# Sums and remainders of the last MLP's weight operands: from VectorE to GpSimd, in a kernel of three fused stages

## The chip, the cores and the metric

One core of one Trainium2 chip. The metric is the device time of one execution in microseconds. The kernel of before took 764.49, 761.42 and 763.99 us in three runs; the median is 763.99 us.

## The reference

Three blocks run one after the other, all in float32. `moe_w_*` and `moe2_w_*` arrive as 64-bit floats, so the kernel also has to turn them into 32-bit ones.

```python
# attention over 32 memory slots: q, k, v of (4, 8, 576, 64), phi of (4, 8, 576, 32)
a = softmax(phi, axis=2)
k_m, v_m = einsum('bhsm,bhsd->bhmd', a, k), einsum('bhsm,bhsd->bhmd', a, v)
x = softmax(q @ k_m.T / 8) @ v_m                 # then as (2304, 512)
x = ((x @ w_a) * (x @ w_b)) @ w_out              # 512 -> 1536 -> 512
h = x @ w2_in                                    # 512 -> 2048
out = maximum(0.01 * h, h) @ w2_out              # 2048 -> 512
```

## The kernel before

Every float32 product is made of three passes in the faster fp32r format: an operand is split into a high part (ScalarE rounds it to fp32r) and a low part (the remainder, value minus high part), and TensorE adds high x high, high x low and low x high.

The program has three stretches on TensorE. In the first (to about 87 us) the attention of the first batch and the first part of the gated MLP run. In the second (to 398 us) the rest of the attention and of the gated MLP run: `wp` (L741, the weights folded with v_m), `ab` (L792), `x1p` (L849). In the third (398 us to the end) the last MLP runs: `h` (L1250) and `o` (L1339, L1320). The last MLP is computed with a Strassen-Winograd scheme: 7 products of half-size blocks in place of 8. For it, sums of blocks of the weights w2_in and w2_out are needed beside the blocks themselves. All of these are made during the second stretch, written to DRAM (`a_scr`) and read back in the third into a ring.

`plan_pair` (L890) plans this work for one pair of 128-row or 128-column blocks, 8 pairs of w2_in ("in") and 8 of w2_out ("out"). For each of the two blocks of a pair there is a load of 512 KB into one of five `stage` places (L255), two ScalarE instructions that take the words of the 64-bit numbers apart (L262, L266) and one VectorE instruction that joins them (L274). Then come four sums per pair (`add`, L935: S1, S2 from S1, S3, S4 from S2, or T1 to T4). Seven operands are then split: ScalarE makes the high part (`high`, L958) and VectorE the low part (`low`, L961). Four stores (L975) follow. So a pair has 4 sums and 7 low parts, 11 VectorE instructions of 128x256 elements, and 16 pairs have 176. All their inputs lie in SBUF.

Four of the "out" pairs are planned early (`SOON`, mp 4 to 7, in the units u = 1 and u = 2 of the gated MLP); one pair waits for the last store of the pair before it, and so do the weights of the second half of the gated MLP after the last of them (`soon[-1:]`, L1011 to L1021). The other twelve pairs follow the last of these stores too (L1026 to L1030).

What comes when is not written by hand: `Plan.order` (L79) is a list scheduler that runs when the program is built. Every step has an engine and a planned cost (`t_dve`, `t_act`, for TensorE a cost per product), the lags between engines are a table (`LAG`), and the due times are passed backwards from TensorE's steps. The planner takes the step that can start first on any engine, and among those that can start equally early on one engine the one that is due first. The order that comes out is fixed: each engine executes its instructions in that order and waits, where an input isn't there, with all that is queued behind. The DMAs of the plan go through one queue, that of SP. On ScalarE the plan's queue also holds the copies that free PSUM banks (`copy`, L809), the high parts of W (L754) and of G (L828); on VectorE the low parts of W (L760) and G (L832) and the products of a and b (L814).

GpSimd has only some memsets and the identity matrix at the start.

Of the kernel before, what the change touches and what calls it, by code (L numbers as in the profile page):

```python
# [9 lines left out]
F32 = mybir.dt.float32  # L10
F32R = mybir.dt.float32r
# [3 lines left out]
ALU = mybir.AluOpType  # L15
AX = mybir.AxisListType

PE, DVE, ACT, DMA = "PE", "DVE", "ACT", "DMA"


class Step:
# [19 lines left out]
class Plan:  # L41
# [4 lines left out]


    LAG = {(PE, PE): 0.0, (DVE, DVE): 0.13, (ACT, ACT): 0.02, (DVE, PE): 0.3}
    LAG.update({(DMA, e): 2.0 for e in (PE, DVE, ACT)})
    LAG.update({(e, DMA): 1.7 for e in (PE, DVE, ACT)})  # L50
    LAG[DMA, DMA] = 2.0
    TICK, BUSY = 3.413, 3100

# [25 lines left out]
    def order(self, idle=None):  # L79

        for x in reversed(self.steps):
            for y in x.then:
                x.latest = min(x.latest, y.latest - self.lag(x, y) - x.cost - x.early)
        for x, r in self.rank.items():
            x.latest = r
        cols = defaultdict(float)

        def slow(t):
            return 1.0 if cols[int(t / self.TICK) - 1] >= self.BUSY else 2.0

        def count(t, cost, share):
            cols[int(t / self.TICK)] += cost * 2400 * share

        blocks, made = [0.0, 0.0], [0]

        def fetched(x):

            return blocks[min((made[0] + x.n - 1) // self.BLOCK, len(blocks) - 1)]

        def issue(x, t):  # L100
            made[0] += x.n
            while made[0] >= self.BLOCK * (len(blocks) - 1):
                blocks.append(t + (self.FETCH if t < self.START else self.FETCH_ALONE))

        free = {PE: 0.85, DVE: 1.0, ACT: 1.0, DMA: 0.8}
        ready = {e: [] for e in free}
        for x in self.steps:
            if not x.waits:
                ready[x.engine].append(x)
        out, left = [], len(self.steps)  # L110
        while left:
            best = None
            for e in free:
                can = []
                for x in ready[e]:
                    at = max(x.ready, free[e], fetched(x) if e == PE else 0.0)
                    if x.take:
                        places = sorted(self.places[x.take[0].pool])
                        if len(places) < len(x.take):
                            continue  # L120
                        at = max(at, places[len(x.take) - 1][0])
                    can.append((at, x))
                if can:
                    first = min(at for at, _ in can)
                    at, x = min((c for c in can if c[0] <= first), key=lambda c: c[1].latest)
                    if best is None or at < best[0]:
                        best = at, x
            if best is None:
                raise RuntimeError("the plan is stuck")
            at, x = best  # L130
            if x.engine == PE and idle is not None:
                until, fillers = idle
                for cost, emit in fillers:
                    while free[PE] + cost * slow(free[PE]) < at and free[PE] + 2 * cost < until:
                        y = Step(PE, cost, emit, n=4)
                        y.start = free[PE]
                        issue(y, y.start)
                        count(free[PE], cost, 1.0)
                        free[PE] += cost * slow(free[PE])
                        out.append(y)  # L140
            ready[x.engine].remove(x)
            left -= 1
            x.start, end = at, at + x.cost * (slow(at) if x.engine == PE else 1)
            if x.engine == PE:
                count(at, x.cost, 0.8)
                issue(x, at)
            free[x.engine] = end
            for h in x.take:
                place = min(self.places[h.pool])
                self.places[h.pool].remove(place)  # L150
                h.place = place[1]
            for h in x.give:
                h.users -= 1
                h.until = max(h.until, end + (1.7 if h.pool == "stage" else 0.2))
                if not h.users:
                    self.places[h.pool].append((h.until, h.place))
            for y in x.then:
                y.waits -= 1
                y.ready = max(y.ready, end + self.lag(x, y))
                if not y.waits:  # L160
                    ready[y.engine].append(y)
            out.append(x)
        return sorted(out, key=lambda x: x.start)


def t_dve(n):

    return 0.1 + n / 950


def t_act(n):

    return 0.08 + n / 1000
# [3 lines left out]
def kernel(  # L177
# [25 lines left out]
    nc = tc.nc  # L203
# [21 lines left out]
    scale = 1.0 / float(D) ** 0.5  # L225
    PASSES = ((0, 0), (0, 1), (1, 0))

    act, dve, pe, dma = nc.scalar, nc.vector, nc.tensor, nc.sync

    keep = ctx.enter_context(tc.tile_pool(name="keep", bufs=1))  # L230
    p_att_cm = tc.tile_pool(name="att", bufs=1, side="right")
# [658 lines left out]
    def plan_pair(kind, mp, due, after, soon):  # L890
# [35 lines left out]
        for n, ops in enumerate(sums):  # L926
            before, users = plan.slot(f"ob{n}")
            for i, (name, x, y, op) in enumerate(ops):

                def add(name=name, x=x, y=y, op=op, n=n, i=i):  # L930
                    if ("t", n) not in c:
                        c["t", n] = keep.tile([128, 2, 2, 128], F32, tag=f"ob{n}", name="S")
                    x, y = (c[z] if isinstance(z, str) else a(*z) for z in (x, y))
                    c[name] = c["t", n][:, i]
                    dve.tensor_tensor(out=c[name], in0=x, in1=y, op=op)  # L935

                need = [made[z] for z in (x, y) if isinstance(z, str)]
                give = [holds[z[0]] for z in (x, y) if not isinstance(z, str)]
                uses = [users] + [made[z].users for z in (x, y) if isinstance(z, str) and made[z].users is not users]
                made[name] = plan.add(DVE, t_dve(256), add, js + before + need, give=give, uses=uses)  # L940
                made[name].users = users
        for i, part in enumerate(parts):
            hold = Hold("stage", 1) if soon else None
            tag = None if soon else f"X{i}" if inner else f"R{i % 2}"
            before, users = ([], []) if soon else plan.slot(tag)
            lows = []
            for o, name in enumerate(part):

                def parted(o, x, i=i):
                    t = c["out", i][:, o]  # L950
                    return t[:, :, x] if inner else t[:, x].rearrange("p (a c) -> p a c", a=2)

                def high(i=i, o=o, name=name, hold=hold, tag=tag, part=part, parted=parted):
                    if o == 0:
                        shape = [128, len(part), 2, 2, 128] if inner else [128, len(part), 2, 256]
                        pool, to = (keep, f"stage{hold.place}") if hold else (p2[0], tag)
                        c["out", i] = pool.tile(shape, F32R, tag=to, name="a_out" if inner else "w2o")
                    act.activation(out=parted(o, 0), in_=src(name), func=ACTF.Copy)  # L958

                def low(o=o, name=name, parted=parted):  # L960
                    dve.tensor_tensor(out=parted(o, 1), in0=src(name), in1=parted(o, 0).bitcast(F32), op=ALU.subtract)  # L961

                direct = name[0] == letter
                need = js if direct else [made[name]]
                uses = [users] if direct else [users, made[name].users]
                hi = plan.add(ACT, t_act(256), high, need + before + lows, uses=uses, take=None if o else hold)
                lows.append(plan.add(
                    DVE, t_dve(256), low, [hi], uses=uses, give=[holds[int(name[1]) - 1]] if direct else ()
                ))

            def store(i=i, part=part):
                shape = [128, len(part), 2, 2, 128] if inner else [128, len(part), 2, 256]
                t = scr.tile(shape, F32, tag=f"{kind}{mp}_{i}", name="a_scr")
                (a_scr if inner else o_scr)[mp, i] = t
                dma.dma_start(out=t, in_=c["out", i].bitcast(F32))  # L975

            kept = plan.add(DMA, 0.73 * len(part), store, lows, uses=[users], give=[hold] if hold else (), due=due)
            (a_kept if inner else o_kept)[mp, i] = kept
            ends.append(kept)
# [507 lines left out]
```

## Time and profile before

| what | value |
|---|---|
| runs | 764.49, 761.42, 763.99 us, median 763.99 |
| profiled execution, its own time | 764.37 us |
| its span, first to last instruction | 762.5 us |
| TensorE matmul busy | 750.5 us, 98% |
| VectorE busy | 549.1 us, 72% |
| ScalarE busy | 423.7 us, 56% |
| GpSimd busy | 1.2 us, 9 instructions |
| granted TensorE clock, mean | 0.997 of 2.4 GHz |

The span is what the profiler saw between the first and the last instruction; the time of the execution is 1.87 us longer. Busy time of an engine is time in which at least one of its instructions was recorded as running. Records of neighbouring instructions on VectorE and ScalarE overlap, so the distance from start to start says more on their rate than the duration of one. GpSimd stands as POOL in the rows, VectorE as DVE, ScalarE as ACT, TensorE as PE, its weight loads as PEld, the queue of DMA issues as SPq.

### The profile page before, as it was taken

What the parts mean: (1) busy time and instruction counts of PE and PEld (TensorE: products, weight loads), DVE (VectorE), ACT (ScalarE), POOL (GpSimd) and SP (SyncE); (2) the same over time, 40 slices, a digit from 0 to 9 for tenths busy, and PEclk for the clock granted to TensorE, in tenths of its full rate; (3) what the DMA queues carried; (4) which work ended last, traced back from release to release, by engine and by line L of the source; (5) the groups of instructions that cost most, each with busy time, mean ns of one, the idle gap of its engine ahead of it and who ended that gap; (6) DMA issues with size and microseconds to landing.
All of it is one profiled execution on the core that took longest, in us unless ns stands there. A gap on an engine that the chain in (4) does not pass through costs nothing.

```text
span 762.5 us, 16527 instructions
## 1 busy us (share of the span) xinstructions
PE 750.5 (98%) x6462; PEld 709.8 (93%) x6462; DVE 549.1 (72%) x1082; ACT 423.7 (56%) x894; POOL 1.2 (0%) x9
## 2 busy tenths in 40 slices
PE   8999999999999999999999999999999999999996
PEld 5599898899898989898999999999999999999996
DVE  5795697786737988897856756976656966756683
ACT  4894575676857676675624455534344734444440
POOL 0000000000000000000000000000000000000000
PEclk9999999999999999999999999999999999999998
DMA  9972547364715596859746777778897788896375
GB/s 312 337 284 88 188 153 264 122 240 152 258 58 166 188 328 229 300 183 328 298 139 221 262 250 250 248 248 255 274 298 253 248 250 248 281 300 205 126 235 139
DMA packets 86926, 175.41 MB, mean 230 GB/s; under 512 B 8000, under 2 KB 35136, under 8 KB 86848
## 3 DMA queue, kind: packets, MB, share of 16 engines
q1 hardware_dynamic: 86608, 174.16, 68.8%
q8 instruction: 51, 0.84, 0.5%
q10 hardware_dynamic: 240, 0.20, 0.1%
q14 instruction: 27, 0.22, 0.1%
HBM read 140.25 MB, written 34.08 MB: 229 GB/s over the span
## 4 chain that ended last, share of the span: by engine, by line
PE 95%; DMA 2%; SPq 1%; DVE 1%; ACT 1%; issue 0%; ACTq 0%
PE h L1250 23%; PE o L1339 22%; PE x1p L849 21%; PE ab L792 20%; PE wp L741 3%; DMA stage<-in_moe_w_a_dram 1%; PE sc L624 1%; PE km L480 1%; PE qT L596 1%; PE warm L1184 1%; PE o L1320 0%; SPq L1375 0%; PE aT L691 0%; DMA w2o<-a_scr 0%; DVE AT L706 0%
## 5 line engine op out<-in xcount | busy, mean ns | idle before, releaser
L1339 PE MATMUL o<-w2o,S 128*128 128x256 f32 x1476 | 198.1, 282 | 0.0
L1339 PEld LDWEIGHTS o<-w2o,S 128*128 128x128 f32 x1476 | 193.0, 190 | 0.0
L792 PEld LDWEIGHTS ab<-AT,W 128*128 128x128 f32 x1152 | 154.2, 188 | 14.9 <-issue 4.2
L849 PE MATMUL x1p<-G,wo 128*128 128x288 f32 x1152 | 163.0, 298 | 0.0
L792 PE MATMUL ab<-AT,W 128*128 128x288 f32 x1152 | 160.8, 297 | 1.0 <-DVE W L760 0.7
L849 PEld LDWEIGHTS x1p<-G,wo 128*128 128x128 f32 x1152 | 154.6, 188 | 6.0 <-DVE x L870 2.5
L1303 DVE TENSOR_TENSOR S<-g,S 128x384 fp32r<-128x384 f32 x168 | 92.9, 556 | 78.5 <-ACT S L1302 78.2
L1302 ACT ACTIVATE S<-g 128x384 fp32r<-128x384 f32 x168 | 87.6, 521 | 99.6 <-PE o L1339 97.4
L1250 PE MATMUL h<-T,ring 128*128 128x384 f32 x720 | 142.2, 336 | 0.0
L1250 PEld LDWEIGHTS h<-T,ring 128*128 128x128 f32 x720 | 121.3, 189 | 0.0
L1250 PE MATMUL h<-B,ring 128*128 128x384 f32 x288 | 57.5, 337 | 0.0
L1293 DVE TENSOR_TENSOR g<-g 128x384 f32<-128x384 f32 x96 | 52.6, 554 | 4.2 <-ACT g L1260 3.0
L814 DVE TENSOR_TENSOR g<-a_sb,ab 128x288 f32<-128x288 f32 x96 | 43.0, 451 | 14.7 <-PE ab L792 10.2
L262 ACT ACTIVATE stage<-stage 128x512 f32<-128x512 f32 x68 | 46.4, 683 | 8.0 <-DMA stage<-in_moe_w_out_dram 3.2
L1250 PEld LDWEIGHTS h<-B,ring 128*128 128x128 f32 x288 | 48.3, 188 | 0.1
L760 DVE TENSOR_TENSOR W<-wp,W 128x512 fp32r<-128x512 f32 x48 | 32.3, 686 | 20.2 <-ACT W L754 19.9
L266 ACT ACTIVATE stage<-stage 128x512 int32<-128x512 uint32 x68 | 46.2, 679 | 0.0
L809 ACT COPY a_sb<-ab 128x288 f32<-128x288 f32 x96 | 38.0, 396 | 12.8 <-PE ab L792 12.3
L754 ACT ACTIVATE W<-wp 128x512 fp32r<-128x512 f32 x48 | 27.9, 597 | 24.5 <-PE wp L741 18.7
L832 DVE TENSOR_TENSOR G<-g,G 128x576 fp32r<-128x576 f32 x48 | 36.2, 755 | 4.6 <-ACT G L828 4.2
L1360 DVE TENSOR_TENSOR C<-C,o 128x768 f32<-128x768 f32 x32 | 30.2, 953 | 12.7 <-PE o L1339 11.3
L1260 ACT ACTIVATE g<-U 128x384 f32<-128x384 f32 x36 | 18.8, 522 | 33.4 <-DVE U L1275 23.7
(108 smaller groups left out, 673.1 us busy)
## 6 DMA issues: line engine op xcount, KB each, us to landing
w2o<-a_scr SPq DMA_DIRECT2D x168, 256.0 KB, 3.5
ring<-a_scr SPq DMA_DIRECT2D x72, 512.0 KB, 4.3
stage<-in_moe_w_out_dram SPq DMA_DIRECT2D x28, 512.0 KB, 5.6
a_scr<-w2o SPq DMA_DIRECT2D x24, 512.0 KB, 5.5
a_scr<-a_out SPq DMA_DIRECT2D x24, 512.0 KB, 5.7
stage<-in_moe_w_in_dram SPq DMA_DIRECT2D x16, 512.0 KB, 4.9
stage<-in_moe_w_a_dram SPq DMA_DIRECT2D x12, 512.0 KB, 6.7
stage<-in_moe_w_b_dram SPq DMA_DIRECT2D x12, 512.0 KB, 6.2
```

Of the source, the lines that this page charges most:

```text
L262: act.activation(out=x, in_=x, func=ACTF.Prelu, scale=2.0 ** -112, alpha=2.0 ** 32)
L266: act.activation(out=self.lw, in_=self.lw.bitcast(U32), func=ACTF.Copy, scale=7.249 / 2.0 ** 32, bias=0.25)
L792: pe.matmul(out=c[x, n][:, :HS], lhsT=W[b, f][:, hw, g, 128 * x:128 * x + 128], rhs=AT[b][:, g, ha, n * HS:(n + 1) * HS], start=(g == 0 an ...
L809: act.copy(c["sb"][:, n], c[0, n][:, :HS])
L814: dve.tensor_tensor(out=c["g"][:, n], in0=c["sb"][:, n], in1=c[1, n][:, :HS], op=ALU.mult)
L832: dve.tensor_tensor(out=t[:, 1], in0=c["g"], in1=t[:, 0].bitcast(F32), op=ALU.subtract)
L849: pe.matmul(out=c[n][:, :HS], lhsT=wo_t[f][:, hw, 128 * m:128 * m + 128], rhs=G[b, f][:, hg, n], start=(f == fs[0] and (hw, hg) == PASSES[0]),
L1250: pe.matmul(out=out, lhsT=ring[i % 2, part][:, o, kp, hw], rhs=x[:, hx], start=fresh and kp == 0 and (hw, hx) == PASSES[0], stop=kp == 1 a ...
L1293: dve.tensor_tensor(out=t, in0=x, in1=y, op=op)
L1302: act.activation(out=t[:, 0], in_=src, func=ACTF.Copy)
L1303: dve.tensor_tensor(out=t[:, 1], in0=src, in1=t[:, 0].bitcast(F32), op=ALU.subtract)
L1339: pe.matmul(out=acc[chain][:, 256 * u:256 * u + 256], lhsT=s[:, hs, 128 * u:128 * u + 128], rhs=t[:, ht], start=fresh and q == 0 and u != ...
```

## The change

GpSimd becomes a fifth engine of the planner with a cost function of its own, and the 4 sums and 7 low parts of every pair are planned and issued on it. Nothing else of the computation changes: the high parts stay on ScalarE, the joins on VectorE, the stores on SP's queue. Since the planner is given other costs and another engine, it may put every step of the plan elsewhere.

```diff
-PE, DVE, ACT, DMA = "PE", "DVE", "ACT", "DMA"
+PE, DVE, ACT, POOL, DMA = "PE", "DVE", "ACT", "POOL", "DMA"
...
-    LAG.update({(DMA, e): 2.0 for e in (PE, DVE, ACT)})
-    LAG.update({(e, DMA): 1.7 for e in (PE, DVE, ACT)})
+    LAG.update({(DMA, e): 2.0 for e in (PE, DVE, ACT, POOL)})
+    LAG.update({(e, DMA): 1.7 for e in (PE, DVE, ACT, POOL)})
...
-        free = {PE: 0.85, DVE: 1.0, ACT: 1.0, DMA: 0.8}
+        free = {PE: 0.85, DVE: 1.0, ACT: 1.0, POOL: 2.0, DMA: 0.8}
...
+def t_pool(n):
+
+    return 0.15 + n / 460
...
-    act, dve, pe, dma = nc.scalar, nc.vector, nc.tensor, nc.sync
+    act, dve, pe, dma, pool = nc.scalar, nc.vector, nc.tensor, nc.sync, nc.gpsimd
...
-                    dve.tensor_tensor(out=c[name], in0=x, in1=y, op=op)
+                    pool.tensor_tensor(out=c[name], in0=x, in1=y, op=op)
...
-                made[name] = plan.add(DVE, t_dve(256), add, js + before + need, give=give, uses=uses)
+                made[name] = plan.add(POOL, t_pool(256), add, js + before + need, give=give, uses=uses)
...
                 def low(o=o, name=name, parted=parted):
-                    dve.tensor_tensor(out=parted(o, 1), in0=src(name), in1=parted(o, 0).bitcast(F32), op=ALU.subtract)
+                    pool.tensor_tensor(out=parted(o, 1), in0=src(name), in1=parted(o, 0).bitcast(F32), op=ALU.subtract)
...
                 lows.append(plan.add(
-                    DVE, t_dve(256), low, [hi], uses=uses, give=[holds[int(name[1]) - 1]] if direct else ()
+                    POOL, t_pool(256), low, [hi], uses=uses, give=[holds[int(name[1]) - 1]] if direct else ()
                 ))
```

The planned cost of one of these instructions goes from t_dve(256) = 0.1 + 256/950 = 0.37 us to t_pool(256) = 0.15 + 256/460 = 0.71 us. These are numbers of the planner's table, not measurements.

## Rows read from the trace of the kernel before

**Rows 1.** The page, part 4: shares of the chain that ended last.

```profile
PE 95%; DMA 2%; SPq 1%; DVE 1%; ACT 1%; issue 0%; ACTq 0%
```

**Rows 2.** Three stretches: us; busy us of PE, PEld, DVE, ACT, POOL; PEclk, DMA share, GB/s.

```profile
0.00:87.00 87.00, 81.64 (x1091) 64.15 (x1092) 61.21 (x116) 55.02 (x113) 1.24 (x9) 1.00 0.72 246
87.00:745.00 658.00, 658.00 (x5300) 635.64 (x5300) 482.75 (x958) 367.62 (x779) 0.00 (x0) 1.00 0.70 230
745.00:762.50 17.50, 10.82 (x75) 9.98 (x73) 5.15 (x9) 1.05 (x2) 0.00 (x0) 0.89 0.53 140
```

**Rows 3.** PE's waits, whole span: us in total, times, longest us.

```profile
PE aT L691 <- DVE AT L706: 0.8, 1, 0.8
...
PE mxT L416 <- DVE mx L406: 0.6, 1, 0.6
```

**Rows 4.** The moved sums (L935) in two stretches: DVE busy us (instructions).

```profile
98.00:182.00 84.00, 6.25 (x16) 1.00 0.59 207
248.00:377.00 129.00, 19.24 (x48) 1.00 0.73 262
```

**Rows 5.** The moved low parts (L961) in the same stretches.

```profile
98.00:182.00 84.00, 11.14 (x28) 1.00 0.59 207
248.00:377.00 129.00, 32.22 (x82) 1.00 0.73 262
```

**Rows 6.** All engines in the later of these stretches, columns as in rows 2.

```profile
248.00:377.00 129.00, 129.00 (x1036) 119.97 (x1036) 112.55 (x260) 87.80 (x203) 0.00 (x0) 1.00 0.73 262
```

**Rows 7.** DVE by time, one pair's last sums and low parts: start us, us.

```profile
161.19 0.71 DVE L274 SCALAR_TENSOR_TENSOR stage<-stage 128x512 int32<-128x512 int32 x1
...
164.14 1.12 DVE L961 TENSOR_TENSOR w2o<-S,w2o 128x256 fp32r<-128x256 f32 x3
165.15 0.45 DVE L961 TENSOR_TENSOR w2o<-stage,w2o 128x256 fp32r<-128x256 f32 x1
...
166.18 0.44 DVE L961 TENSOR_TENSOR w2o<-stage,w2o 128x256 fp32r<-128x256 f32 x1
```

**Rows 8.** GpSimd's groups by shape: busy us, mean ns of one.

```profile
L1177 POOL MEMSET kk<- 128x256 f32 x2 | 0.6, 313 | 0.0
masks.py:199 POOL TENSOR_SCALAR_AFFINE_SELECT ident<-ident 128x128 f32<-128x128 f32 x1 | 0.3, 293 | 0.0
masks.py:197 POOL MEMSET ident<- 128x128 f32 x1 | 0.2, 204 | 0.0
```

**Rows 9.** DVE's groups by shape, 248 to 377 us, two with both inputs in SBUF.

```profile
L274 DVE SCALAR_TENSOR_TENSOR stage<-stage 128x512 int32<-128x512 int32 x22 | 15.1, 687 | 0.1
L832 DVE TENSOR_TENSOR G<-g,G 128x576 fp32r<-128x576 f32 x19 | 14.3, 751 | 1.5 <-ACT G L828 1.5
```

**Rows 10.** ACT by time: a high part that waited for a sum.

```profile
260.67 0.42 ACT L958 ACTIVATE w2o<-S 128x256 fp32r<-128x256 f32 x1 [3.20 <-DVE S L935]
```

**Rows 11.** DVE by time: a low part of W.

```profile
279.62 0.68 DVE L760 TENSOR_TENSOR W<-wp,W 128x512 fp32r<-128x512 f32 x1
```

**Rows 12.** PE by time, the block whose second half uses this W.

```profile
278.41 6.64 PE L792 MATMUL ab<-AT,W 128*128 128x288 f32 x48
```

**Rows 13.** SP's queue by time: the last stores of pairs, the ring's loads.

```profile
375.25 3.80 SPq L975 DMA_DIRECT2D a_scr<-a_out  x4
379.10 1.29 SPq L1053 DMA_DIRECT2D ring<-a_scr  x2
```

**Rows 14.** DMA issues, 370 to 400 us: KB each, median us to landing.

```profile
ring<-a_scr SPq DMA_DIRECT2D x2, 256.0 KB, 4.4
```

**Rows 15.** PE by time, the start of the last MLP.

```profile
398.48 2.24 PE L1250 MATMUL h<-B,ring 128*128 128x384 f32 x12
```

**Rows 16.** SP by time, the first weight load behind the early pairs.

```profile
168.20 1.90 SPq L255 DMA_DIRECT2D stage<-in_moe_w_a_dram  x1
```

**Rows 17.** PE by time, the first product that needs these weights.

```profile
226.35 1.09 PE L741 MATMUL wp<-wab,vblk 64*32 64x512 f32 x16
```

More of the change, by code (lines that the diff above doesn't have):

```diff
@@ L955, in high @@
                         shape = [128, len(part), 2, 2, 128] if inner else [128, len(part), 2, 256]
-                        pool, to = (keep, f"stage{hold.place}") if hold else (p2[0], tag)
-                        c["out", i] = pool.tile(shape, F32R, tag=to, name="a_out" if inner else "w2o")
+                        home, to = (keep, f"stage{hold.place}") if hold else (p2[0], tag)
+                        c["out", i] = home.tile(shape, F32R, tag=to, name="a_out" if inner else "w2o")
                     act.activation(out=parted(o, 0), in_=src(name), func=ACTF.Copy)
                 def low(o=o, name=name, parted=parted):
-                    dve.tensor_tensor(out=parted(o, 1), in0=src(name), in1=parted(o, 0).bitcast(F32), op=ALU.subtract)
+                    pool.tensor_tensor(out=parted(o, 1), in0=src(name), in1=parted(o, 0).bitcast(F32), op=ALU.subtract)
                 direct = name[0] == letter
```

## The prediction

> **What bounds the kernel now.** I read the chain of waits first: 95% of it is TensorE [rows 1]. Then the busy time by stretches [rows 2]: from 87 to 745 us TensorE is busy for 658.00 of 658.00 us, at a granted clock of 1.00, the level of 2.4 GHz. Its idle time lies outside: 87 - 81.64 = 5.4 us before 87 us, and 17.5 - 10.82 = 6.7 us in the tail. Then its waits: VectorE is named as releaser in four before the tail, from 0.8 down to 0.6 us, 2.7 us in sum [rows 3]; all of them end before 87 us. So in the stretch of 658 us TensorE waits for nothing, and what it has to do there isn't touched by the change.
>
> Next I looked for the instructions that move. The sums fall into two stretches, 16 at 98 to 182 us and 48 at 248 to 377 us [rows 4], the low parts with 28 and 82 [rows 5]; that is 174 of 176, and all of them lie within TensorE's 658 us. In the later stretch VectorE is busy for 112.55 of 129 us and ScalarE for 87.80, while TensorE is busy for all of it [rows 6]. VectorE is nearly full there, and still not what TensorE waits for.
>
> **What the change removes.** Three low parts in a row start at 164.14 and the next at 165.15 us, so one occupies VectorE for 0.337 us [rows 7]. 176 of them are 59 us, 130 x 0.337 = 43.8 us of it in the later stretch. On the path that sets the end this is worth 0 us: the work that hides it is TensorE's unbroken stream, and the bound of the gain is what TensorE waits for VectorE there, 0 us.
>
> **What it adds.** No row of before shows a GpSimd instruction with two inputs. From below: a write alone of the same size takes 0.313 us [rows 8]. In between an estimate: two memsets of 128 and 256 elements take 204 and 313 ns, so 0.85 ns per element and 95 ns fixed; one instruction with a read and a write takes 293 ns for 128 elements, (293 - 95) / 128 = 1.55 ns, so a read adds 0.70 [rows 8]. Two reads and a write of 256 elements are then 95 + 256 x 2.25 = 671 ns. From above: the same plus a wait for the whole of the longest VectorE instruction with two SBUF inputs in this stretch, 0.751 us [rows 9], 1.42 us. I take 0.67 us, because it rests on the only rows of this engine. GpSimd then has 44 x 0.67 = 29 us of work in the 84 us of the early stretch and 130 x 0.67 = 87 us in the 129 us of the later one, 68%. The planner books 0.707 us for each, 92 us. At the lower end it would be 41 us, at the upper 185 us, more than there is.
>
> Each moved step is one instruction and issues no DMA. GpSimd's own queue holds nothing else after the first microseconds, so nothing there is passed or held up. But the waits change: ScalarE waits for a sum before it makes its high part, and SP's queue waits for the low parts before a store. Behind the waiting ScalarE instruction stand the copies that free PSUM banks, the high parts of W and G and the word instructions; behind a store stand the loads of the next pair. One wait of this sort exists already: a high part waits 3.20 us for a VectorE sum [rows 10], and TensorE goes on. That was while `x1p` ran; while `ab` runs the cover is thinner. The low part of a W ends at 279.62 + 0.68 = 280.30 us [rows 11], and the products that use it are the second 24 of a block that begins at 278.41 us with 6.64 / 48 = 0.138 us each, so at 281.7 us [rows 12]. That is 1.4 us of slack. A ScalarE that loses more than this against its plan stops TensorE.
>
> At the end of the stretch the cover is thick: the last stores of the pairs are issued by 375.25 + 3.80 = 379.1 us, the last two ring loads by 380.4 us [rows 13], 4.4 us later they land [rows 14], at 384.8 us, and the last MLP starts at 398.48 us [rows 15], 13.7 us of slack. The early pairs release the weight loads at 168.20 us [rows 16], and the product that needs these weights starts at 226.35 us [rows 17]. From the last join to the last low part a pair takes 166.62 - 161.19 = 5.4 us on VectorE [rows 7]; on GpSimd 11 x 0.67 = 7.4 us, 2 us later. This vanishes in 58 us.
>
> **The sum.** Gain on the path 0 us, loss on the path 0 us as long as GpSimd keeps to the planner's 0.707 us: 764.37 us, the profiled execution's own time (its span of 762.5 us and 1.87 us around it). The median of the three runs is 763.99 us, 0.4 us lower, and the runs differ by 3.1 us. About 0.5%, 3.8 us, is what a measurement of this kernel can tell from no change.
>
> **One rule against the change.** Rows first: in the later stretch VectorE has 22 joins of 687 ns and 19 low parts of G of 751 ns, 29.4 us with both inputs in SBUF [rows 9]; no row shows GpSimd reading beside them. Of such pairs the Trainium skill, "SBUF — State Buffer", section "Who interferes with whom", says that the second read port of VectorE is GpSimd's, and that of a VectorE instruction with two SBUF inputs and a GpSimd instruction that reads SBUF the second to come is held until the first is done. By it the time would be that of the first rival; without it that of the sum. Nothing in this trace decides between them.
>
> **The rivals.**
>
> GpSimd becomes the pace (slower). Place: 248 to 377 us. If the two engines shut each other out, GpSimd stands still while one of these VectorE instructions runs. It is at work 68% of the time, so 0.68 x 29.4 = 20 us are added to its 130 instructions, 0.154 us each: 0.825 us, 0.118 us over what the planner booked, 15.3 us in all. If the pairs keep their present pace, the planner leaves GpSimd 129 - 92 = 37 us idle, and this swallows it. If the planner, with VectorE relieved, packs the pairs as closely as GpSimd's booked cost allows, little idle time is left to swallow it; ScalarE falls behind by up to 15.3 us, and TensorE stops for what is over 1.4 us: 13.9 us, 778 us. With half of it swallowed, 7.7 - 1.4 = 6.3 us: 771 us. It decides from where GpSimd's mean instruction exceeds 0.707 us while it works without a break. For it: VectorE's 87% here show that pairs are packed onto whatever is free. Against it: a wait of 3.2 us that cost nothing, and a planner that books 5% more than my estimate. VectorE, held in its turn for some 0.34 us by 68% of 41 instructions, loses 9.5 us and stays far below what it gave up. At the upper bound of 1.42 us the stretch would need 185 us, 56 us more than it has.
>
> The planner gives back early waits (faster). With other costs every step may be put elsewhere. If the four early waits for VectorE went, 761.7 us, still within 0.5%; all 5.4 us of early idle time, 759.0 us. Against it: no moved instruction comes before 98 us.
>
> The change doesn't do what it says: the inputs of all moved instructions lie in SBUF, and I see nothing that would keep them off GpSimd. The time would be 764.4 us too, without a chance of its own.
>
> **How the numbers follow.** No measurable change: 0.61. GpSimd's pace: 0.33, from 768.3 us (just over 0.5%) to 778 us and the far bound beyond, about 0.13 of it above 772 us. Faster: 0.06, nearly all below 761.4 us. The range of 761.4 to 772 us leaves out some 0.18; its lower end is the lowest run of before. Taken alone, the likeliest case has 761.4 to 768.
>
> **What would show it.** Right: 176 GpSimd instructions of 0.6 to 0.75 us from start to start, VectorE's busy time lower by some 60 to 70 us (its records are longer than its occupation), TensorE busy without a break from 87 to 745 us, `h` beginning at 398 us within 1 us. Wrong by the first rival: waits of ScalarE for GpSimd of over 1.4 us, with TensorE waiting for W or a PSUM bank just behind them, and `h` later by the loss. The prediction is also wrong if TensorE's products get another pitch than 0.138 us, which I hold fixed, or if GpSimd's low parts come so late that the ring's loads land after 398 us.

## The result, and the profile after the change

The changed kernel takes 768.14 us in the median (767.73 to 769.80), beside 762.78 us of the kernel before on the same chip. The ratio of the two kernels' runs is 1.0062 with a 95% interval of 1.0042 to 1.0083: slower by some 4.7 us (the medians, of four runs each, lie 5.4 us apart). The profiled execution took 767.73 us, with a span of 765.9 us.

The page of the changed kernel, parts 1 and 4, answers to [rows 1]:

```profile
PE 753.5 (98%) x6462; PEld 711.2 (93%) x6462; DVE 506.5 (66%) x906; ACT 424.1 (55%) x894; POOL 148.7 (19%) x185
...
PE 82%; DMA 5%; POOL 4%; issue 3%; DVE 2%; ACT 2%; SPq 0%; POOLq 0%; DVEq 0%; ACTq 0%
```

GpSimd is now in the chain that ended last, and TensorE's share fell from 95% to 82%. Busy time by stretches, columns as in [rows 2]; the third and fourth lines answer to [rows 2, 6]:

```profile
0.00:240.00 240.00, 234.79 (x2679) 205.48 (x2680) 155.91 (x288) 158.14 (x341) 36.15 (x53) 1.00 0.60 203
...
87.00:240.00 153.00, 152.83 (x1589) 140.97 (x1588) 94.69 (x172) 103.14 (x228) 34.90 (x44) 1.00 0.53 179
...
87.00:745.00 658.00, 655.90 (x5262) 631.80 (x5261) 436.81 (x777) 365.94 (x775) 147.43 (x176) 1.00 0.69 229
...
248.00:377.00 129.00, 127.29 (x1006) 116.42 (x1005) 78.75 (x126) 85.41 (x194) 103.48 (x121) 1.00 0.73 259
```

TensorE is no longer unbroken, and the break lies in the later stretch: 1.7 us of idle time there, 0.2 us between 87 and 240 us. From 248 to 377 us VectorE fell from 112.55 to 78.75 us busy and GpSimd rose from 0 to 103.48 us, 80% of the stretch. The granted clock is 1.00 as before. TensorE by time, beside [rows 15]:

```profile
402.96 1.21 PE L1255 MATMUL h<-B,ring 128*128 128x384 f32 x6
```

The last MLP begins 4.48 us later than at 398.48, and from there on nothing is lost: its first and last product lie 323.04 us apart, 323.03 before. So nearly all of the loss is in the pairs' later stretch. (The two profiled executions lie only 3.4 us apart, because the tail behind the last `h` is 1.1 us shorter in this one: 765.9 - 726.00 against 762.5 - 721.51 us.) GpSimd's groups by shape, busy us and mean ns of one:

```profile
L940 POOL TENSOR_TENSOR S<-stage 128x256 f32<-128x256 f32 x32 | 29.9, 938 | 226.8 <-DVE stage L279 225.3 <-POOL w2o L966 1.4
L966 POOL TENSOR_TENSOR a_out<-S,a_out 128x256 fp32r<-128x256 f32 x32 | 26.7, 855 | 0.1
L966 POOL TENSOR_TENSOR w2o<-S,w2o 128x256 fp32r<-128x256 f32 x32 | 26.0, 820 | 7.3 <-ACT w2o L963 7.3
```

The records average 805 to 953 ns over all seven groups. From start to start, where one follows the other without a wait, the median is 0.71 us and the mean 0.84 us. So half of them take about what the planner books (0.707 us), and the rest draw the mean 0.13 us above it. VectorE's two operations with both inputs in SBUF, 248 to 377 us, answer to [rows 9]:

```profile
L279 DVE SCALAR_TENSOR_TENSOR stage<-stage 128x512 int32<-128x512 int32 x23 | 19.5, 848 | 12.0 <-ACT stage L271 9.4 <-POOL S L940 1.2 <-POOL w2o L966 1.2
...
L837 DVE TENSOR_TENSOR G<-g,G 128x576 fp32r<-128x576 f32 x18 | 18.1, 1006 | 5.8 <-ACT G L833 5.7
```

They were 687 and 751 ns long and are 848 and 1006 ns now, with nothing in their own shape or operands changed.

**How VectorE stops TensorE.** One place, three engines by time: first VectorE, then GpSimd, then TensorE.

```profile
320.83 1.05 DVE L1098 TENSOR_TENSOR T<-x 128x384 f32<-128x384 f32 x1
321.81 1.10 DVE L1098 TENSOR_TENSOR T<-x,x 128x384 f32<-128x384 f32 x1
322.83 1.23 DVE L279 SCALAR_TENSOR_TENSOR stage<-stage 128x512 int32<-128x512 int32 x1
323.99 0.74 DVE L837 TENSOR_TENSOR G<-g,G 128x576 fp32r<-128x576 f32 x1
324.65 0.68 DVE L765 TENSOR_TENSOR W<-wp,W 128x512 fp32r<-128x512 f32 x1
```

```profile
318.38 0.74 POOL L966 TENSOR_TENSOR w2o<-S,w2o 128x256 fp32r<-128x256 f32 x1
...
321.41 2.10 POOL L940 TENSOR_TENSOR S<-stage,S 128x256 f32<-128x256 f32 x2
```

```profile
325.38 1.60 PE L797 MATMUL ab<-AT,W 128*128 128x288 f32 x10 [0.36 <-DVE W L765]
327.23 2.20 PE L797 MATMUL ab<-AT,W 128*128 128x288 f32 x12 [0.25 <-DVE g L819]
```

GpSimd's two sums take 2.10 us where two at its ordinary pace (the first of its lines) take 1.4. Beside them VectorE's sums over `x` take 1.05 and 1.10 us and the join 1.23 us. In the kernel before a join takes 0.69 us [rows 9], and the two sums:

```profile
317.35 0.55 DVE L1093 TENSOR_TENSOR T<-x 128x384 f32<-128x384 f32 x1
317.82 0.55 DVE L1093 TENSOR_TENSOR T<-x,x 128x384 f32<-128x384 f32 x1
```

Together the three take 0.50 + 0.55 + 0.54 = 1.6 us more. W's low part behind them in VectorE's fixed order is late too, and TensorE waits for it.

**How ScalarE's queue stops TensorE.** ScalarE's waits, 240 to 400 us: us in total, times, longest.

```profile
ACT stage L267 <- DMA stage<-in_moe_w_in_dram: 11.5, 10, 2.5
ACT a_out L963 <- POOL S L940: 9.9, 9, 3.2
ACT w2o L963 <- POOL S L940: 8.4, 5, 5.1
```

One of the first kind, ScalarE by time, and the product behind it:

```profile
280.19 0.68 ACT L267 ACTIVATE stage<-stage 128x512 f32<-128x512 f32 x1 [1.39 <-DMA stage<-in_moe_w_in_dram]
280.77 0.57 ACT L759 ACTIVATE W<-wp 128x512 fp32r<-128x512 f32 x1
281.25 0.67 ACT L833 ACTIVATE G<-g 128x576 fp32r<-128x576 f32 x1
281.82 0.39 ACT L814 COPY a_sb<-ab 128x288 f32<-128x288 f32 x1
```

```profile
282.26 0.93 PE L797 MATMUL ab<-AT,W 128*128 128x288 f32 x5 [0.25 <-ACT a_sb L814]
```

ScalarE stands at a word instruction until its load lands, and the high parts of W and G and the copy that frees a PSUM bank stand behind it. The load is late because SP's queue, which issues it, waits for GpSimd's low parts: at stores (L980), and at loads (L260) whose `stage` place a low part has to free. This load itself waited 1.0 us for one, and the load ahead of it 2.9 us.

```profile
SPq L980 <- POOL w2o L966: 24.4, 11, 5.4
SPq L980 <- POOL a_out L966: 24.0, 7, 10.4
SPq L260 <- POOL a_out L966: 12.6, 8, 2.9
```

(SP's waits, 240 to 350 us.) In the kernel before SP waited no less at its stores, for VectorE's low parts:

```profile
SPq L975 <- DVE a_out L961: 36.1, 14, 9.3
SPq L975 <- DVE w2o L961: 20.3, 10, 6.7
```

So SP's waits aren't new, and in sum no longer than before. What rose are ScalarE's waits (240 to 400 us): for loads from 5.2 to 13.7 us, for sums from 12.0 to 18.3 us.

### The profile page after: what moved, and what is told of

Its sections match the earlier page's. It is cut to its first block, busy times and chain, and to the rows that moved or that the text cites. A ratio compares the mean times of both kernels' runs of the same rounds, so it can differ in the third digit from the quotient of the medians.

```text
span 765.9 us, 16608 instructions
## 1 busy us (share of the span) xinstructions
PE 753.5 (98%) x6462; PEld 711.2 (93%) x6462; DVE 506.5 (66%) x906; ACT 424.1 (55%) x894; POOL 148.7 (19%) x185
## 4 chain that ended last, share of the span: by engine, by line
PE 82%; DMA 5%; POOL 4%; issue 3%; DVE 2%; ACT 2%; SPq 0%; POOLq 0%; DVEq 0%; ACTq 0%
PE h L1255 23%; PE o L1344 22%; PE x1p L854 15%; PE ab L797 14%; DMA stage<-in_moe_w_in_dram 2%; PE wp L746 2%; POOL a_out L966 2%; POOL S L940 2%; DMA stage<-in_moe_w_a_dram 1%; PE sc L629 1%; PE km L485 1%; DMA stage<-in_moe_w_out_dram 1%; PE o L1325 1%; PE qT L601 1%; PE warm L1189 1%
## 5 line engine op out<-in xcount | busy, mean ns | idle before, releaser
L940 POOL TENSOR_TENSOR S<-stage 128x256 f32<-128x256 f32 x32 | 29.9, 938 | 226.8 <-DVE stage L279 225.3
L837 DVE TENSOR_TENSOR G<-g,G 128x576 fp32r<-128x576 f32 x48 | 43.5, 906 | 15.9 <-ACT G L833 15.7
L279 DVE SCALAR_TENSOR_TENSOR stage<-stage 128x512 int32<-128x512 int32 x44 | 34.3, 779 | 16.1 <-ACT stage L271 12.6
```

Source lines behind the costliest of these rows:

```text
L837: dve.tensor_tensor(out=t[:, 1], in0=c["g"], in1=t[:, 0].bitcast(F32), op=ALU.subtract)
L940: pool.tensor_tensor(out=c[name], in0=x, in1=y, op=op)
```

## The experiments

Three theories are named in the expectations. **A**: GpSimd's steps are longer than the planner booked, and the lateness passes through the queues. **B**: GpSimd and VectorE hold each other up wherever both read two inputs from SBUF. **C**: the new order of steps costs by itself.

Each kernel was run 4 to 12 times beside the kernel before on the same chip. Besides the ratio, one figure is read from the profile of one execution, the time lost before the last MLP: the start of the first `h`, less TensorE's idle time from 0 to 240 us, against the same in the kernel before, 398.48 - 5.36 = 393.12 us. For the changed kernel it is 402.96 - (240 - 234.79) - 393.12 = 4.6 us. The profile shows 1.9 us of this as idle time of TensorE (the ends of matmuls are modelled), so I read the starts and not the gaps.

This figure leaves out what is lost before 240 us. It can be read from starts alone: two products `wp` begin at 97.20 and 226.35 us in the kernel before [rows 17], and the first `h` at 398.48 us. In the changed kernel (first line) and in the last of the table:

```profile
226.48 1.09 PE L746 MATMUL wp<-wab,vblk 64*32 64x512 f32 x16
...
226.50 1.09 PE L746 MATMUL wp<-wab,vblk 64*32 64x512 f32 x16
399.14 2.24 PE L1259 MATMUL h<-B,ring 128*128 128x384 f32 x12
```

From the second `wp` to `h` the changed kernel loses 4.35 us and the last kernel 0.5; between the two `wp` (the first at 96.89 and 96.28 us) they lose 0.4 and 1.1 us. For the other kernels this reading differs from the column by at most 0.8 us.

```
kernel            GpSimd's step   ratio [95%]                lost before h
changed           0.84 us mean    1.0062 [1.0042, 1.0083]    4.6
e1 old order      -               1.0041 [1.0025, 1.0057]    3.0
e2 write once     0.26            0.9999 [0.9988, 1.0011]    0.4
e3 write thrice   0.995           1.0085 [1.0069, 1.0102]    7.6
e4 booked 0.91    -               1.0020 [1.0010, 1.0031]    0.4
e5 sums           -               1.0070 [1.0043, 1.0097]    3.4
e6 low parts      -               1.0023 [1.0010, 1.0036]    1.5
e7 write 0.85     0.85            0.9999 [0.9987, 1.0011]    0.3
e8 early only     -               1.0015 [1.0002, 1.0029]    0.2
e9 read first     0.97            1.0107 [1.0094, 1.0120]    9.3
e10 booked 0.84   -               1.0025 [1.0011, 1.0040]    2.4
e11 booked both   -               1.0018 [1.0008, 1.0029]    0.3
e12 read first    0.84            1.0016 [1.0002, 1.0030]    0.9
```

**1. Is it the order or the instructions?** The first keeps the changed kernel's GpSimd instructions, and books them on VectorE as before, so that the order stays the old one:

```diff
-made[name] = plan.add(POOL, t_pool(256), add, ...)
+made[name] = plan.add(DVE, t_dve(256), add, ...)
...
-    POOL, t_pool(256), low, [hi], ...
+    DVE, t_dve(256), low, [hi], ...
```

> The planner orders everything as in the kernel before (the moved steps are planned on VectorE at 0.37 us), and GpSimd executes the 176 moved instructions at their old places. Theory A (GpSimd's instructions are longer than booked, by themselves or by exclusion with VectorE, and what waits for them in fixed queues stops TensorE): clearly slower than the changed kernel, since now 0.37 us is booked for what takes 0.8 to 0.9; above 772 us. Theory C (the new order alone is to blame): as the kernel before, 761 to 765 us.

The second keeps the new order and has each of the 176 steps only write its 256 elements, once. It leaves out the sums and remainders, and with them the reading and the waits for their inputs:

```diff
-pool.tensor_tensor(out=c[name], in0=x, in1=y, op=op)
+pool.memset(c[name], 0.5)
...
-pool.tensor_tensor(out=parted(o, 1), in0=src(name), in1=..., op=ALU.subtract)
+pool.memset(parted(o, 1).bitcast(F32), 0.001)
```

> The order of the changed kernel; in place of each of the 176 sums and low parts GpSimd writes a constant over the same 256 elements once (about 0.3 us, no reading). It leaves out the sums and remainders of the last MLP's weights. Theories A and B (what counts is GpSimd's length, or its exclusion with VectorE): as the kernel before, 761 to 765 us, TensorE without a wait from 90 to 745 us. Theory C (the new order): as the changed kernel, about 768 us.

The new order with short writes loses nothing that can be measured, so C falls. The old order with the GpSimd instructions loses 3.0 us: not more than with the new order, as A had it. Whether it is less the ratios don't tell (their intervals overlap), and why it isn't more no run shows.

**2. Which pairs?** Only the 44 instructions of the early pairs go to GpSimd:

```diff
-pool.tensor_tensor(...)
+(pool if soon else dve).tensor_tensor(...)
```

(in both places, and the booking likewise.)

> Only the 44 sums and low parts of the four early pairs go to GpSimd, the other 132 stay on VectorE. If the loss sits where the pairs are packed, after 248 us: as the kernel before, 762 to 765 us, and TensorE waits for nothing from 90 to 745 us. If every GpSimd instruction costs its share wherever it lies: a quarter of the loss, 1 to 1.5 us, too little to tell from none.

0.2 us are lost, and TensorE's idle time from 240 us to `h` is 0; between the two `wp` the time is that of the kernel before within 0.1 us. The ratio of 1.0015 is 1.1 us, with an interval from 0.2 to 2.2 us: as much as a quarter of the loss, which the second forecast had, so the times alone don't decide. The starts do, for the one execution: the early pairs are not where the loss is.

**3. Length without reading.** As in the second kernel, but with three writes per step (here for the sums; the low parts likewise, in all cuts below):

```diff
-pool.tensor_tensor(out=c[name], in0=x, in1=y, op=op)
+pool.memset(c[name], 0.5)
+pool.memset(c[name], 0.5)
+pool.memset(c[name], 0.5)
```

> As the run before it, but each constant is written three times over, so that a step occupies GpSimd for 0.8 to 0.95 us, as long as in the changed kernel, without reading from SBUF. It leaves out the sums and remainders of the last MLP's weights. Theory B (GpSimd and the VectorE instructions with two SBUF inputs hold each other up): most of the loss goes, 762 to 765 us, and the low parts of G are back at 0.75 us. Theory A (GpSimd's length against what the planner booked): the loss stays, 767 to 772 us. Theory C: 768 us.

and with the third cut to 80 elements:

```diff
-pool.memset(c[name], 0.5)
+pool.memset(c[name][:, :, :40], 0.5)
```

> The order of the changed kernel; each of the 176 steps writes its constant over 256, 256 and 80 elements, about 0.84 us from step to step, the mean that the changed kernel has, without reading. It leaves out the sums and remainders of the last MLP's weights. Theory A (GpSimd's length against what was booked is enough): 766 to 769 us. Theory B (the exclusion of the two engines is needed for the loss, since it also lengthens VectorE's own instructions): 762 to 765 us.

At 0.995 us a step 7.6 us are lost (A's forecast), at 0.85 us none that can be measured (B's). Length can cost by itself, but not at the changed kernel's mean. This doesn't settle it, since these writes don't wait for joins and high parts, and so can run ahead. VectorE is undisturbed in both, as this group of the kernel with 0.85 us shows (its mean is 751 ns in [rows 9]):

```profile
L837 DVE TENSOR_TENSOR G<-g,G 128x576 fp32r<-128x576 f32 x48 | 36.3, 756 | 16.6 <-ACT G L833 16.4
```

**4. Half of the move.** Sums on GpSimd and low parts on VectorE, and the reverse:

```diff
-    pool.tensor_tensor(out=parted(o, 1), ...)
+    dve.tensor_tensor(out=parted(o, 1), ...)
...
-    POOL, t_pool(256), low, [hi], ...
+    DVE, t_dve(256), low, [hi], ...
```

> Only the 64 sums go to GpSimd, the 112 low parts stay on VectorE. Theory A: GpSimd has 48 instructions in the later stretch, some 43 of 129 us, so it is idle between them and no lateness adds up: 762 to 765 us. Theory B: every GpSimd instruction can still hold up a low part of G or a join, a third of the loss stays: 764 to 766 us.

> Only the 112 low parts go to GpSimd, the 64 sums stay on VectorE. Theory A: 82 instructions in the later stretch, some 70 of 129 us; lateness adds up in bursts only: 763 to 766 us. Theory B: two thirds of the loss stay: 765 to 767 us.

With 64 instructions on GpSimd, and GpSimd busy for some 60 us in all, as much is lost by the ratio as with 176. Neither theory had that. (Its six runs spread from 766.57 to 772.78 us, and the profile is that of the quickest, with 3.4 us lost; where the slower ones lose the rest isn't known.) VectorE's groups of this kernel say where it went:

```profile
L966 DVE TENSOR_TENSOR w2o<-stage,w2o 128x256 fp32r<-128x256 f32 x24 | 17.5, 735 | 0.8 <-ACT w2o L963 0.7
...
L966 DVE TENSOR_TENSOR a_out<-stage,a_out 128x256 fp32r<-128x256 f32 x24 | 14.5, 612 | 0.5 <-ACT a_out L963 0.4
```

Such a low part takes 0.44 to 0.45 us on VectorE beside an idle GpSimd [rows 7]; here 0.735 and 0.612. Every low part kept on VectorE has two inputs in SBUF and meets GpSimd's sums. This speaks for B: few GpSimd instructions beside a VectorE that has much work of this kind cost as much as many. It doesn't rule out A, since GpSimd's sums are longer too: their three groups average 881 to 991 ns. The reverse split loses 1.5 us; both forecasts cover its time.

**5. Booking.** GpSimd's steps booked at 0.91 us:

```diff
-    return 0.15 + n / 460
+    return 0.35 + n / 460
```

> The changed kernel, with the planner booking 0.35 + 256/460 = 0.91 us for each moved instruction, a little more than the 0.87 us measured. Theory A (longer than booked): the waits are planned for, TensorE's waits from 87 to 745 us go, 762 to 765 us. Theory B (exclusion also lengthens VectorE's own instructions, and no booking on GpSimd repairs that): part of the loss stays, 764 to 768 us. Theory C makes no forecast; it would see about 768 us.

at 0.84 us, its measured mean (0.28 in place of 0.35):

> The changed kernel with 0.28 + 256/460 = 0.84 us booked, the measured mean from start to start. Theory A: the waits of TensorE go, and the pairs end earlier than with 0.91 us booked: 763 to 765 us. Theory B: bursts in which GpSimd and VectorE meet are still longer than booked, and VectorE's own lengthening isn't booked: 765 to 768 us.

and at 0.84 us with VectorE's lengthened instructions booked too:

```diff
+    return 0.28 + n / 460
...
-        lo = plan.add(DVE, t_dve(576), low, ...)
+        lo = plan.add(DVE, t_dve(576) + 0.15, low, ...)
...
-            js.append(plan.add(DVE, t_dve(512), conv.join, [v, z]))
+            js.append(plan.add(DVE, t_dve(512) + 0.1, conv.join, [v, z]))
```

> As the run before it, and VectorE's low parts of G booked 0.15 us longer, the joins of the pairs 0.1 us, as the trace of the changed kernel shows them. Theory B: the planner now knows both sides of the exclusion on average, 763 to 765 us, below the run before it. Theory A: no difference to the run before it.

Against 4.6 us, 2.4 us are lost before `h` with 0.84 booked, 0.4 with 0.91 and 0.3 with both engines booked. But with 0.91 and with both engines booked something is lost behind: the first and last `h` lie 324.5 and 324.4 us apart, 1.4 us more than the 323.03 before (323.3 with 0.84). With 0.91 the pairs end at 394 us and not at 386, and what was put off for them falls into the first microseconds of the last MLP, where VectorE is busy for 18.00 of 22 us, after 14.08 before (the kernel with 0.91, then the kernel before):

```profile
398.00:420.00 22.00, 21.70 (x124) 20.39 (x123) 18.00 (x36) 11.14 (x24) 0.00 (x0) 1.00 0.84 270
398.00:420.00 22.00, 22.00 (x129) 21.86 (x129) 14.08 (x26) 9.35 (x19) 0.00 (x0) 1.00 0.61 199
```

So an honest booking moves the loss and shrinks it to about 0.2%; it doesn't make it vanish. ScalarE's waits for loads and sums (240 to 400 us) are no shorter with 0.91 than in the changed kernel, 32.8 us against 32.0: their sum doesn't tell the loss. The ratios of the two kernels with 0.84 don't differ beyond their intervals, so the forecasts that set them apart stay undecided. Each booking also sorts all steps anew, so the series is not only one of doses.

**6. Length with the waits kept, and hardly any reading.** Each step reads 8 elements of both its inputs, so that it waits as the real one does, and then writes twice. The sums and remainders are left out:

```diff
-pool.tensor_tensor(out=c[name], in0=x, in1=y, op=op)
+pool.tensor_tensor(out=c[name][:, :, :4], in0=x[:, :, :4], in1=y[:, :, :4], op=op)
+pool.memset(c[name], 0.5)
+pool.memset(c[name], 0.5)
```

> The order of the changed kernel; each of the 176 steps first does its sum or difference for 8 of the 256 elements, so that it waits for the same inputs as before, and then writes a constant twice over all 256: 0.8 to 0.9 us a step, of which only a short piece reads. It leaves out most of the sums and remainders of the last MLP's weights. Theory A (length alone, against what was booked): 766 to 769 us, as the changed kernel. Theory B (the exclusion of GpSimd and VectorE): 762 to 765 us, the low parts of G at 0.76 to 0.80 us.

That came out at 0.97 us a step. With the second write cut to 104 elements a step has the changed kernel's own mean of 0.84 us:

```diff
-pool.memset(c[name], 0.5)
+pool.memset(c[name][:, :, :52], 0.5)
```

> As the run that reads 8 elements and then writes twice (0.91 us a step, 0.97 on average), with the second write cut to 104 elements: 0.84 us on average, the mean of the changed kernel, with the same inputs waited for and hardly any reading beside VectorE. It leaves out most of the sums and remainders of the last MLP's weights. Theory A (GpSimd's length against the 0.707 us booked): 767 to 769 us, as the changed kernel, with the low parts of G at 0.76 us. If VectorE's own lengthening had a share of its own: in between, 764 to 767 us.

At 0.97 us 9.3 us are lost, twice the changed kernel's loss and more than either forecast had, so A's mechanism is real and steep. At the changed kernel's own mean 0.9 us are lost, a fifth (by the ratio 1.2 of 4.7 us, a quarter): the forecast for the case that VectorE's lengthening has a share of its own. ScalarE's waits of this last kernel (240 to 400 us) and VectorE's group:

```profile
ACT w2o L965 <- POOL S L942: 10.8, 6, 4.5
ACT a_out L965 <- POOL S L942: 8.9, 8, 2.9
ACT stage L267 <- DMA stage<-in_moe_w_in_dram: 8.8, 7, 2.2
```

```profile
L837 DVE TENSOR_TENSOR G<-g,G 128x576 fp32r<-128x576 f32 x48 | 36.3, 755 | 17.7 <-ACT G L833 17.6
```

ScalarE waits as long for GpSimd's sums as in the changed kernel, 19.7 us against 18.3, and a little less for loads. What differs is VectorE: 755 ns where the changed kernel has 906 over the whole run:

```profile
L837 DVE TENSOR_TENSOR G<-g,G 128x576 fp32r<-128x576 f32 x48 | 43.5, 906 | 15.9 <-ACT G L833 15.7
```

GpSimd isn't undisturbed: its reads of 8 elements take 0.20 us in the median and up to 1.02 us.

**What follows.** Neither part suffices at this size. GpSimd's mean length with VectorE undisturbed loses 0.9 us before `h` (0.16%); the mutual delay with GpSimd's lateness booked loses 0.4 us before it and 1.4 us behind (0.20%). Together they lose 4.6 us (0.62%). My reading, which no run isolates: GpSimd's lateness uses up the slack of ScalarE's and SP's queues, and a VectorE that is itself late has none left to give. One thing stays open. The last kernel has the same mean with fewer long steps: of those that follow each other without a wait from 248 to 377 us, 10 of 113 take over 1.1 us, and 25 of 111 in the changed kernel. Whether these bursts or VectorE's own lengthening make up the difference isn't separated. No version was faster than the kernel before, and none could be expected to be by much: TensorE has no break there to give back.

## Why the prediction was right or wrong, step by step

The time lies in the range only because the range took in the first rival. The likeliest case, no change at 764.4 us, didn't come; the rival did, priced at 771 us with half of the lateness swallowed, measured at 768.14. That is even just under the rival's lower edge of 768.3 us, since the kernel before ran at 762.78 us in this comparison and not at 764.37. The rival's signs came: ScalarE waits for GpSimd of up to 5.1 us, TensorE waiting for W and for a PSUM bank, `h` later by 4.48 us.

- **Gain 0 us: right.** 176 instructions left VectorE and TensorE gained nothing. VectorE's busy time fell from 549.1 to 506.5 us, by 42.6 and not by 60 to 70; the records of the instructions that stayed grew by 13.4 us in all.
- **GpSimd's instruction, 0.67 us from memsets: right for an undisturbed one.** GpSimd by time in the kernel with 0.91 us booked, where VectorE left it alone:

```profile
387.18 0.75 POOL L966 TENSOR_TENSOR a_out<-stage,a_out 128x256 fp32r<-128x256 f32 x1
387.88 0.75 POOL L940 TENSOR_TENSOR S<-S,stage 128x256 f32<-128x256 f32 x1
388.59 0.86 POOL L940 TENSOR_TENSOR S<-stage 128x256 f32<-128x256 f32 x1
389.41 0.75 POOL L966 TENSOR_TENSOR a_out<-stage,a_out 128x256 fp32r<-128x256 f32 x1
```

  From start to start 0.70, 0.71 and, for the sum of two inputs out of `stage`, 0.82 us. The planner's 0.707 is good for this state.
- **"Loss on the path 0 us as long as GpSimd keeps to the planner's 0.707 us": the step at which the likeliest case failed.** The condition was not met: the mean is 0.84 us. The rival's working had 0.825 from 20 us of exclusion over 130 instructions. That this is so near is in part luck: instructions that meet none of VectorE's with both inputs in SBUF follow each other in 0.72 us in the mean and not in 0.67, and the exclusion adds 0.12 us in the mean and not 0.154. I had the number and still gave the case 0.33, on the grounds that a wait of 3.20 us had cost nothing [rows 10] and that the planner booked 5% more than my estimate. Neither reason bears on the exclusion.
- **The rule.** VectorE's G low parts take 0.75 us where no GpSimd instruction runs beside them, and 1.07 us in the median, up to 1.48, where one does; GpSimd's take 0.74 undisturbed and 1.0 to 1.2 in the median beside such a VectorE instruction. VectorE's instructions with an input in PSUM keep their length (W's low part 0.68 us before and after), and GpSimd's pure writes leave VectorE at 755 ns. The Trainium skill, "SBUF — State Buffer", section "Who interferes with whom", has the rule behind all four, without these times; the trace agrees with each.
- **"VectorE loses 9.5 us and stays far below what it gave up": size right, use wrong.** From 248 to 377 us L837 gained 0.255 us on 18 instructions and L279 0.161 us on 23, 8.3 us in all. Some of the sums over `x`, which the working had left out, took twice as long (0.55 us before, 1.05 and 1.10 us in the example). But a sum over the stretch says nothing about a fixed order: the instructions just ahead of W's low part were held up, and TensorE stood until 325.38 us, with VectorE only 61% busy over the stretch.
- **The rival's price: half of the mechanism, and a size too large.** The rival let only GpSimd's lateness reach TensorE, through ScalarE; at the same mean and with VectorE undisturbed that loses 0.9 us, so most of the loss needs what the rival left aside. Lateness of (0.84 - 0.707) x 121 = 16 us, 15.3 predicted; 4.6 us of it reached TensorE and not 6.3. The share that idle time swallows was a guess of one half; it was about 0.6 after the slack of 1.4 us, (16 - 1.4 - 4.6) / 16, if all of the loss is counted as GpSimd's.
- **The end and the early pairs: right.** The last ring loads are issued by 389.1 us (380.4 before), and 4.4 us of landing still leave 9 us to `h`. With the early pairs alone on GpSimd 0.2 us were lost before `h`.
- **The pitch of 0.138 us** stayed, and the clock too.

## What to carry to other kernels

Before work is moved from VectorE to GpSimd, list what stays on VectorE with both inputs in SBUF beside it: those instructions and the moved ones stretch each other (here 0.75 to 0.91 us and 0.72 to 0.84 us in the mean), and costs taken from either engine alone are too low. In a fixed order, as here, a spare 40% of an engine need not absorb this; look at the instruction right ahead of the one that TensorE waits for, and at what stands behind each new wait. Where TensorE is unbroken, such a move has nothing to win: none of the thirteen kernels here was faster than the kernel before.

## What was not expected

- Moving 64 instructions cost as much as moving 176 (1.0070 against 1.0062). The low parts that stayed on VectorE went from 0.45 us to a mean of up to 0.735 us.
- Between 0.84 and 0.97 us a step, with the same waits and VectorE undisturbed, the loss went from 0.9 to 9.3 us: 0.13 us x 121 steps is 16 us more work for GpSimd in the stretch, and half of that came out as TensorE's loss.
- Writes without waits, at 0.85 us a step, cost nothing (0.9999), and at 0.995 us 7.6 us.
